# Attention, then experts: the order of GpSimd's instructions, token numbers inside the sorted rows, two heads per block for the last queries, and fp16 scalars in the bias layer

## The chip, the cores and the metric

The kernel runs on one core of a Trainium2 chip. The engines of the core work side by side, each through its own queue of instructions: TensorE (PE, matmuls; PEld its weight loads), VectorE (DVE), ScalarE (ACT), GpSimd (POOL) and SyncE (SP). In this kernel POOL and SP also issue the DMA transfers. The metric is the time of one execution on the device in microseconds; lower is better.

## What is computed

Eight batches of eight heads with 576 tokens and 64 values per head go through softmax attention with an additive bias; the bias comes from a small two-layer network on the logarithm of the distance of two tokens. The result of each token, a row of 512 values, then goes through one of eight experts, which its domain id names.

```python
rel = pos[:, None] - pos[None, :]
x = (log1p(abs(rel)) / log1p(maximum(pos[:, None], 1)))[..., None]
bias = maximum(x @ w1 + b1, 0) @ w2            # hidden width 32, one value per head
scores = q @ k.T / sqrt(64) + bias             # per batch and head, 576 x 576
attn = softmax(scores) @ v
x = attn.transpose(0, 2, 1, 3).reshape(4608, 512)
for e in range(8):                             # domain_id: 4608 numbers 0..7
    m = domain_id == e
    out[m] = maximum(x[m] @ w1[e], 0) @ w2[e]  # 512 -> 1024 -> 512
```

## The kernel before, in words

**Setup** (`_setup_constants`, L67 to L108) builds a table L of logarithms of distances (128 partitions: 32 hidden units for each of four query positions), a `slope` column for each group of four queries and the negated bias `nb`. **The bias phase** (`_phase_bias`) runs over nine blocks of 64 queries. For each, VectorE makes 16 tiles `hr` (L126: a window of L times a column of `slope`, then the maximum with `nb`), TensorE multiplies each by W2BIG into `eb` (L136; L141 for the last 64 keys, twice, once for each half of the partitions), and ScalarE moves `eb` out as exp(bias), or as the plain bias for some parts (L150, L153, L156).

**Routing** (`_phase_route`) gives each token a slot: expert e owns slots 640e to 640e + 639, in five chunks of 128, and a loop for an overflow beyond that is not entered with these data. VectorE counts in a chain of small operations that begins with the matmul `app` (L207) and ends with `posi` (L276), the slot of each token. Forty indirect DMAs on GpSimd (L287) then scatter the token numbers into `fire_perm`, an array in HBM, and SyncE loads that back as `sidx` (L292).

**Attention** (`_Attention.run`) takes 21 units for each batch: TensorE computes the scores of 128 keys by 512 queries for two heads (or some other 1024-wide piece), ScalarE takes the exp (L412), VectorE multiplies it by exp(bias) (L417), and TensorE multiplies with v (`av`) into `pu`. `norm` divides by the sum. Five indirect DMAs on GpSimd (L477) put the batch's rows, in fp16, into their slots in `fire_x`. q, k and v of batch b + 2 are ordered from HBM at unit 1 of batch b, also through GpSimd; a DMA from an fp32 array into an fp16 tile converts. p = 4 in `av` and `norm` are the last 64 queries.

**The experts** (`_phase_moe`): one DMA on SyncE fetches the 640 rows of an expert (`xg`, L578), TensorE transposes them (L559), then the first layer (`hps`, L601), Relu on ScalarE (L605) and the second layer (`ops`, L566). VectorE copies `ops` to `res` (L569, four buffers) and GpSimd scatters `res` to the output (L570) by `sidx`. Weights of experts 0 to 2 are loaded during attention, those of experts 3 to 6 by eight DMAs in a row at the start of the experts, those of expert 7 after expert 0.

The order of instructions on PE, DVE and ACT is that of the program. On POOL and SP the scheduler chooses it.

Of the kernel before, what the change touches and what calls it, by code (L numbers as in the profile page):

```python
# [9 lines left out]
F32 = mybir.dt.float32  # L10
# [6 lines left out]
P = 128  # L17
S = 576
# [12 lines left out]
PAD = 1 << 20  # L31

# [23 lines left out]
def _no_order(tc, key, inst):  # L56

    ins = inst.ins if hasattr(inst, "ins") else inst
    tc.declare_no_dep(ins, group=key, reason="rows of one permutation")
    tc.add_to_no_dep_group(key, ins)  # L60


def _setup_constants(tc, G, w1, b1, w2):
# [12 lines left out]
    nc.sync.dma_start(out=w1col, in_=bass.AP(tensor=w1.tensor, offset=0, ap=[[0, 4], [1, 32], [1, 1]]))  # L76
    G.nb1 = cst.tile([P, 1], F32, tag="nb1", name="nb1")
    nc.sync.dma_start(out=G.nb1, in_=bass.AP(tensor=b1.tensor, offset=0, ap=[[0, 4], [1, 32], [1, 1]]))
    nc.vector.tensor_scalar(out=G.nb1, in0=G.nb1, scalar1=-1.0, scalar2=None, op0=AO.mult)
# [9 lines left out]
    si = cst.tile([P, NGR], I32, tag="si", name="si")  # L89
    li = G.tmp.tile([P, W4 + W1], I32, tag="li", name="li")  # L90
    for g in range(4):
        pg = slice(32 * g, 32 * g + 32)

        nc.gpsimd.iota(si[pg, 0:128], base=4 * g, channel_multiplier=0, pattern=[[1, 4], [16, 32]])
        nc.gpsimd.iota(si[pg, 128:144], base=512 + g, channel_multiplier=0, pattern=[[4, 16]])
        nc.gpsimd.iota(li[pg, 0:W4], base=-(C4 + 4 * g), channel_multiplier=0, pattern=[[1, W4]])
        nc.gpsimd.iota(li[pg, W4:], base=-(C1 + 512 + g), channel_multiplier=0, pattern=[[1, W1]])
    G.slope = cst.tile([P, NGR], F32, tag="slope", name="slope")
    nc.vector.tensor_copy(out=G.slope, in_=si)
    nc.vector.tensor_scalar(out=G.slope, in0=G.slope, scalar1=1.0, scalar2=None, op0=AO.max)  # L100
    nc.scalar.activation(out=G.slope, in_=G.slope, func=AF.Ln, bias=1.0, scale=1.0)
    nc.vector.reciprocal(out=G.slope, in_=G.slope)
    nc.vector.tensor_scalar(out=G.slope, in0=G.slope, scalar1=w1col[:], scalar2=None, op0=AO.mult)
    lf = G.tmp.tile([P, W4 + W1], F32, tag="lf", name="lf")
    nc.vector.tensor_copy(out=lf, in_=li)
    nc.vector.scalar_tensor_tensor(out=lf, in0=lf, scalar=-1.0, in1=lf, op0=AO.mult, op1=AO.max)
    G.L4 = cst.tile([P, W4 + W1], F16, tag="L4", name="L4")
    nc.scalar.activation(out=G.L4, in_=lf, func=AF.Ln, bias=1.0, scale=1.0)  # L108


def _phase_bias(tc, G):
# [3 lines left out]
    with tc.tile_pool(name="fsb", bufs=1, side="right") as fsb, \  # L115
         tc.tile_pool(name="fps", bufs=1, space=bass.MemoryType.PSUM) as fps:
        for ib in range(9):
            hrl = []
            for k16 in range(16):
# [3 lines left out]
                else:  # L123
                    m, c0 = 128 + k16, W4 + C1 - 4 * k16
                hr = fsb.tile([P, S], F16, tag="hr", name="hr", bufs=36)
                nc.vector.tensor_scalar(out=hr, in0=G.L4[:, c0: c0 + S],  # L126
                                        scalar1=G.slope[:, m: m + 1], scalar2=G.nb1[:],
                                        op0=AO.mult, op1=AO.max)
                hrl.append(hr)
            for jcs in ((0, 1), (2, 3), (4,)):  # L130
                eb = fps.tile([P, 2, 512], F32, tag="eb", name="eb", bufs=3)
                for k16 in range(16):
                    for lj, jc in enumerate(jcs):
                        hr = hrl[k16]
                        if jc < 4:
                            nc.tensor.matmul(out=eb[:, lj, 32 * k16: 32 * k16 + 32],  # L136
                                             lhsT=rap(hr, jc, [[4, 128]]),
                                             rhs=G.W2BIG[:, 0:32], start=True, stop=True)
                        else:
                            for h2 in range(2):  # L140
                                nc.tensor.matmul(  # L141
                                    out=eb[64 * h2: 64 * h2 + 64, lj, 32 * k16: 32 * k16 + 32],
                                    lhsT=hr[:, 512:576], rhs=G.W2BIG[:, 0:32], start=True, stop=True)
                ebv = eb.rearrange("p l (i h) -> p l h i", h=8)
                i0 = 64 * ib
                if jcs[0] == 4:
                    for h2 in range(2):
                        o = G.biasR[64 * h2: 64 * h2 + 64, :, i0: i0 + 64] if ib < 8 else \
                            G.biasRL[64 * h2: 64 * h2 + 64]
                        nc.scalar.activation(out=o, in_=ebv[64 * h2: 64 * h2 + 64, 0, h2::2, :],  # L150
# [16 lines left out]
def _phase_route(tc, G, moe_domain_id):  # L167
# [8 lines left out]
    G.perm_dram = nc.dram_tensor("fire_perm", (NSLOT, 1), I32, kind="Internal").ap()  # L176
# [563 lines left out]
```

## Time and profile before

| | |
|---|---|
| median of 3 runs | 527.84 us (526.59 to 532.48) |
| the profiled execution | 523.68 us, its span 522.0 us |
| busy in the span | PE 373.6 us (72%), DVE 260.3 (50%), ACT 231.1 (44%), POOL 202.0 (39%) |
| mean granted clock of TensorE | 0.896 of full speed |
| stages | setup to 16 us, bias to 70, routing to 88, attention to 321, experts to 514, end 522 |

The profile was taken in one execution, and its times are counted from the start of its span. Busy shares are means over stages that have different limits, so the table alone does not say what a change in one stage is worth.

### The profile page before, as it was taken

The numbers are of one execution on the slowest core, as the hardware profiler recorded it, in microseconds if no ns is written. First come the engines' busy times: TensorE is split into PE (matmuls) and PEld (weight loads), VectorE is DVE, ScalarE is ACT, GpSimd is POOL, SyncE is SP. The second block draws the span as 40 slices with busy tenths as digits, with TensorE's granted clock in tenths as the row PEclk, the third lists the DMA queues.
The fourth block names the chain that finished last, engine by engine and source line by source line (L and its number), as shares of the span: only waits on it lengthen the run. The fifth ranks groups of instructions, "written<-read, shape, count | busy, mean of one in ns | idle before, by whom it ended". The sixth has DMA issues, their size and how long they took to land. (4 is left out here: it accounts for less than half of the span.)

```text
span 522.0 us, 10886 instructions
## 1 busy us (share of the span) xinstructions
PE 373.6 (72%) x4578; PEld 235.3 (45%) x4578; DVE 260.3 (50%) x572; ACT 231.1 (44%) x290; POOL 202.0 (39%) x238
## 2 busy tenths in 40 slices
PE   0578844311298988889898977079639999999992
PEld 0366733100055555465555544055425566566550
DVE  5899985100369695777768674013022422422411
ACT  1444521000388987889697875021402143143140
POOL 9740445777606546543403042603013303313312
PEclk9999999555599999999897989579959999999997
DMA  0999987000992999979401010899998313102211
GB/s 3 155 233 366 319 123 131 2 0 0 99 155 53 161 203 149 151 124 114 77 3 46 4 46 21 160 241 241 215 246 206 112 50 123 69 22 88 81 39 73
DMA packets 79034, 61.39 MB, mean 118 GB/s; under 512 B 23558, under 2 KB 71430, under 8 KB 78984
## 3 DMA queue, kind: packets, MB, share of 16 engines
q0 software_dynamic: 56576, 45.12, 49.7%
q1 hardware_dynamic: 22408, 15.57, 10.8%
q8 instruction: 36, 0.59, 0.4%
q14 instruction: 14, 0.11, 0.1%
HBM read 67.17 MB, written 25.49 MB: 177 GB/s over the span
## 5 line engine op out<-in xcount | busy, mean ns | idle before, releaser
L412 ACT ACTIVATE e<-sc 128x1024 f16<-128x1024 f32 x168 | 156.7, 998 | 93.5 <-remote 67.2
L605 ACT ACTIVATE hT<-hps 128x640 f16<-128x640 f32 x64 | 45.1, 704 | 137.8 <-PE hps L601 136.2
L570 POOL DMA_INDIRECT out_dram<-res,sidx x40 | 39.5, 988 | 132.6 <-DVE res L569 131.9
L566 PE MATMUL ops<-w2e,hT 128*128 128x512 f16 x320 | 71.5, 383 | 0.0
L601 PE MATMUL hps<-xT,w1e 128*128 128x320 f16 x512 | 71.2, 300 | 0.0
L385 PE MATMUL sc<-qkT 64*128 64x512 f16 x256 | 54.3, 407 | 22.7 <-ACT e L412 16.7
L477 POOL DMA_INDIRECT fire_x<-xt,posi x32 | 34.4, 1076 | 81.2 <-DVE xt L459 71.0
L569 DVE COPY res<-ops 128x512 f32<-128x512 f32 x40 | 27.7, 691 | 76.2 <-PE ops L566 51.0
L417 DVE TENSOR_TENSOR e<-e,biasM 128x1024 f16<-128x1024 f16 x96 | 63.4, 685 | 3.3 <-ACT e L412 3.0
L601 PEld LDWEIGHTS <-w1e 128*128 128x128 f16 x512 | 50.3, 98 | 20.7
L136 PE MATMUL eb<-W2BIG,hr 128*128 128x32 f16 x576 | 36.0, 196 | 25.8 <-DVE hr L126 18.8
L433 PE MATMUL pu<-vext,e 128*128 128x65 f16 x1024 | 53.0, 199 | 0.0
L126 DVE TENSOR_SCALAR hr<-L,slope,nb 128x576 f16<-128x576 f16 x144 | 51.6, 435 | 1.7 <-ACT L L108 1.7
L561 DVE COPY xT<-pxt 128x512 f16<-128x512 f16 x40 | 15.8, 421 | 65.8 <-PE pxt L559 64.1
L566 PEld LDWEIGHTS <-hT 128*128 128x128 f16 x320 | 31.3, 99 | 36.8 <-issue 1.4
L287 POOL DMA_INDIRECT fire_perm<-nidx,posi x40 | 38.7, 969 | 21.0 <-issue 21.0
L433 PEld LDWEIGHTS <-e 128*128 128x128 f16 x1024 | 46.2, 102 | 0.0
L367 DVE COPY qkT<-pt 128x1024 f16<-128x1024 f16 x32 | 21.8, 683 | 47.7 <-remote 43.5
L136 PEld LDWEIGHTS <-hr 128*128 128x128 f16 x576 | 26.5, 117 | 34.7 <-DVE hr L126 17.6
L429 PE MATMUL pu<-vrag,e 128*128 128x130 f16 x128 | 29.9, 234 | 13.1 <-DVE xl L470 7.9
L559 PE MATMUL pxt<-idn,xg 128*128 128x128 f16 x160 | 15.1, 235 | 33.6 <-DMA xg<-fire_x 18.1
L345 PE MATMUL pt<-idn,qn 128*64 128x128 f16 x256 | 15.3, 249 | 27.1 <-DVE qkT L367 14.3
(123 smaller groups left out, 407.6 us busy)
## 6 DMA issues: line engine op xcount, KB each, us to landing
fire_x<-zero SPq DMA_DIRECT2D x1, 9984.0 KB, 37.0
w1e<-in_moe_w_dram POOLq DMA_DIRECT2D x8, 1024.0 KB
w2e<-in_moe_w_dram POOLq DMA_DIRECT2D x8, 1024.0 KB
xg<-fire_x SPq DMA_DIRECT2D x8, 640.0 KB, 8.6
qn<-in_q_dram POOLq DMA_DIRECT2D x8, 512.0 KB
kn<-in_k_dram POOLq DMA_DIRECT2D x8, 512.0 KB
vst<-in_v_dram POOLq DMA_DIRECT2D x8, 512.0 KB
fire_perm<-nidx,posi POOLq DMA_INDIRECT x40
```

What stands on the lines that cost most here:

```text
L126: nc.vector.tensor_scalar(out=hr, in0=G.L4[:, c0: c0 + S], scalar1=G.slope[:, m: m + 1], scalar2=G.nb1[:], op0=AO.mult, op1=AO.max)
L136: nc.tensor.matmul(out=eb[:, lj, 32 * k16: 32 * k16 + 32], lhsT=rap(hr, jc, [[4, 128]]), rhs=G.W2BIG[:, 0:32], start=True, stop=True)
L287: _no_order(tc, "slots", nc.gpsimd.indirect_dma_start(out=G.perm_dram[:, :], out_offset=bass.IndirectOffsetOnAxis(ap=G.posi[0:n, c:c + 1], ...
L385: mm(out=sc[:, h2, :], lhsT=self.qkT[b, p][hs[h2], 1, 128 * c: 128 * c + 128], rhs=self.qkT[b, p][hs[h2], 0, :], start=not raw, stop=True)
L412: nc.scalar.activation(out=ef[:, 0:n], in_=sf[:, 0:n], func=AF.Exp, bias=0.0, scale=0.125)
L417: self.nc.vector.tensor_tensor(out=job[0], in0=job[0], in1=job[1], op=AO.mult)
L433: mm(out=self.pu[:, c // 2, o + 65 * h2: o + 65 * h2 + 65], lhsT=self.e[b, ("m", p, j)][:, h2, 128 * c: 128 * c + 128], rhs=vx[:, 2 * p + ...
L477: _no_order(self.tc, "x_rows", self.nc.gpsimd.indirect_dma_start(out=self.x_dram[:, :], out_offset=bass.IndirectOffsetOnAxis(ap=self.G.pos ...
L566: nc.tensor.matmul(out=ops_, lhsT=hT[:, fc, t0: t0 + 128], rhs=w2e[:, fc, :], start=(fc == 0), stop=(fc == 7))
L570: _no_order(tc, "out_rows", nc.gpsimd.indirect_dma_start(out=out[:], out_offset=bass.IndirectOffsetOnAxis(ap=idx, axis=0), in_=res[:], in_ ...
L601: nc.tensor.matmul(out=hps[:, hf, 0:HC], lhsT=w1e[:, dc, 128 * fc: 128 * fc + 128], rhs=xT[:, dc, HC * hf: HC * hf + HC], start=(dc == 0), ...
L605: nc.scalar.activation(out=hT[:, fc, :].rearrange("p (a b) -> p a b", a=2), in_=hps[:, :, 0:HC], func=AF.Relu, bias=0.0, scale=1.0)
```

## The change

On **GpSimd**, a helper `_Issue` fixes the order of loads, token iotas, weights and scatters to that of the program; scatters that follow each other stay free among themselves. The **forty L287 scatters** go, and with them `fire_perm` and `sidx`: rows of `fire_x` are now 514 wide, and the last four bytes hold the token number, which a small iota on GpSimd writes into `xt` and `xl` (`new_rows`). Slots that no token fills get PAD with the zero fill. The out scatter takes its row numbers from `xg` itself.

`xg` is fetched as **five DMAs of 128 rows** per expert, two experts ahead. **Weights** of expert e + 3 are loaded behind the first out scatter of expert e; `res` has six buffers. The program orders the weights of experts 0, 1 and 2 at unit 13 of batches 1, 2 and 3, as before; GpSimd now keeps to that place.

For the **last 64 queries**, one matmul takes two heads of the queries as its 128 rows and two heads of v: 20 in place of 36 per batch; `norm` divides 128 x 512 in one operation. In the **bias phase**, 27 of the 144 `hr` tiles move to ScalarE (Relu with scale and bias), the other 117 take their two pointer scalars as fp16 copies, and the last 64 keys need one matmul per tile, not two. **Setup** uses fewer, wider iotas, takes the absolute value on ScalarE, and does the table in two parts.

```diff
+class _Issue:
+    def __call__(self, inst):
+        ins = _ins(inst)
+        for before in self.free or ([self.fixed] if self.fixed is not None else []):
+            self._behind(ins, before)
+        self.fixed, self.free = ins, []
+        return inst
+    def scatter(self, inst):
+        ins = _ins(inst)
+        if self.fixed is not None:
+            self._behind(ins, self.fixed)
+        self.free.append(ins)
+        return inst
...
+    G.slope16 = cst.tile([P, NGR], F16, tag="slope16", name="slope16")
+    nc.vector.tensor_copy(out=G.slope16, in_=G.slope)
...
+    nc.scalar.activation(out=lf[:, W4:], in_=li[:, W4:], func=AF.Abs, bias=gs[:, 2:3], scale=1.0)
+    nc.scalar.activation(out=G.L4[:, W4:], in_=lf[:, W4:], func=AF.Ln, bias=1.0, scale=1.0)
...
-                nc.vector.tensor_scalar(out=hr, in0=G.L4[:, c0: c0 + S],
-                                        scalar1=G.slope[:, m: m + 1], scalar2=G.nb1[:],
-                                        op0=AO.mult, op1=AO.max)
+                if k16 in (3, 8, 13):
+                    nc.scalar.activation(out=hr, in_=G.L4[:, c0: c0 + S], func=AF.Relu,
+                                         bias=G.pb1[:], scale=G.slope[:, m: m + 1])
+                else:
+                    nc.vector.tensor_scalar(out=hr, in0=G.L4[:, c0: c0 + S],
+                                            scalar1=G.slope16[:, m: m + 1], scalar2=G.nb16[:],
+                                            op0=AO.mult, op1=AO.max)
...
-    for bb in range(B):
-        for t in range(NT):
-            n = 128 if t < 4 else 64
-            c = NT * bb + t
-            _no_order(tc, "slots", nc.gpsimd.indirect_dma_start(
-                out=G.perm_dram[:, :],
-                out_offset=bass.IndirectOffsetOnAxis(ap=G.posi[0:n, c:c + 1], axis=0),
-                in_=nidx[0:n, bb, t:t + 1], in_offset=None))
...
+            out = self.pu[:, h2, o: o + 130].rearrange("p (q d) -> p q d", q=2)
+            mm(out=out, lhsT=ex[:, 0, 64 * q: 64 * q + 128],
+               rhs=vr[:, q: q + 2, 65 * h2: 65 * h2 + 65], start=True, stop=False, skip_group_check=True)
+            for j in range(4):
+                l0 = 256 * (j % 2) + 64 * q
+                mm(out=out, lhsT=self.e[b, ("l", j // 2)][:, h2, l0: l0 + 128],
+                   rhs=vx[:, 2 * q + h2: 2 * q + h2 + 3: 2, j, :], start=False, stop=(j == 3),
+                   skip_group_check=True)
...
+    def new_rows(self, tag, n, c, base, step):
+
+        t = self.G.asb.tile([n, c, XW], F16, tag=tag, name=tag, bufs=2)
+        self.G.issue(self.nc.gpsimd.iota(t[:, :, DM:].bitcast(I32), base=base, channel_multiplier=step,
+                                         pattern=[[1, c], [0, 1]]))
+        return t
...
-        xg = msb.tile([P, NCH, DM], F16, tag="xg", name="xg", bufs=3)
-        nc.sync.dma_start(out=xg, in_=x_dram[e * CAP: e * CAP + CAP, :]
-                          .rearrange("(k p) d -> p k d", p=128))
...
+            xg = msb.tile([P, XW], F16, tag="xg", name="xg", bufs=4 * NCH)
+            r0 = e * CAP + 128 * kk
+            nc.sync.dma_start(out=xg, in_=x_dram[r0: r0 + 128, :])
...
-        if e == 0:
-            for e2 in range(G.NW, min(E, G.NW + G.NW2)):
-                G.wts[e2] = _load_expert(nc, G.wsb2, moe_w1, moe_w2, e2, G.NW2)
...
-            second(hT, 128 * kk, w2e, G.sidx[:, e * NCH + kk, :])
-        if e + G.NW + G.NW2 < E:
-            G.wts[e + G.NW + G.NW2] = _load_expert(nc, G.wsb, moe_w1, moe_w2, e + G.NW + G.NW2, G.NW)
+            second(hT, 128 * kk, w2e, xgs[e][kk][:, DM:])
+            if kk == 0 and e + G.NW < E:
+                e2 = e + G.NW
+                pool, n = (G.wsb2, G.NW2) if e < G.NW2 else (G.wsb, G.NW)
+                G.wts[e2] = _load_expert(nc, pool, moe_w1, moe_w2, e2, n, G.issue)
```

On GpSimd, after routing, this stands before (qn, ql, kn, kl and vst are q, k and v of a batch and their last 64 tokens, vrag the last tokens of v; the first qn is that of batch 2):

```order
L287 DMA fire_perm<-nidx,posi 9984x1 x40
L323 DMA qn<-in_q_dram 128x8x256
L323 DMA kn<-in_k_dram 128x8x256
L331 DMA vst<-in_v_dram 128x8x256
L323 DMA qn<-in_q_dram 128x8x256
```

And this now, on the same engine in the same place:

```order
L301 MEMSET pb 128x672
L359 DMA qn<-in_q_dram 128x8x256
L362 DMA ql<-in_q_dram 64x8x64
L359 DMA kn<-in_k_dram 128x8x256
L362 DMA kl<-in_k_dram 64x8x64
L369 DMA vst<-in_v_dram 128x8x256
L376 DMA vrag_134<-in_v_dram 64x4x64 x2
L520 IOTA xt 128x4
L359 DMA qn<-in_q_dram 128x8x256
```

The loads of batch 2, and those of batch 3 that begin in the last row, follow the memory fills of routing; nothing that takes `posi` stands ahead of them.

On GpSimd, at the start of the experts, the last rows of weights and the out scatters stand so before (w1e and w2e are the two layers of an expert):

```order
L543 DMA w2e<-in_moe_w_dram 128x8x512
L570 DMA out_dram<-res,sidx 4608x512 x4
L541 DMA w1e<-in_moe_w_dram 128x4x1024
L570 DMA out_dram<-res,sidx 4608x512
L543 DMA w2e<-in_moe_w_dram 128x8x512
L570 DMA out_dram<-res,sidx 4608x512 x35
```

And so now, from the last sorted rows on:

```order
L526 DMA fire_x<-xl,posi 9984x514
L617 DMA out_dram<-res,xg 4608x512
L592 DMA w1e<-in_moe_w_dram 128x4x1024
L594 DMA w2e<-in_moe_w_dram 128x8x512
L617 DMA out_dram<-res,xg 4608x512 x5
L592 DMA w1e<-in_moe_w_dram 128x4x1024
L594 DMA w2e<-in_moe_w_dram 128x8x512
L617 DMA out_dram<-res,xg 4608x512 x5
```

The weights come in pairs, with five out scatters between two pairs; before, the eight loads stood ahead of the first out scatter.

## Rows read from the trace of the kernel before

**Rows 1.** Windows: us, busy (instructions) PE, PEld, DVE, ACT, POOL; PEclk, DMA share, GB/s

```profile
0.00:16.00 16.00, 0.00 (x0) 0.00 (x0) 8.35 (x11) 3.25 (x4) 14.72 (x39) 1.00 0.15 11
16.00:70.00 54.00, 44.23 (x866) 34.97 (x866) 52.96 (x149) 25.32 (x54) 21.58 (x25) 1.00 1.15 258
91.00:139.00 48.00, 7.52 (x60) 3.86 (x57) 3.00 (x5) 2.08 (x3) 35.20 (x37) 0.50 0.12 12
139.00:321.00 182.00, 158.40 (x2511) 96.28 (x2511) 134.87 (x278) 152.65 (x164) 68.45 (x73) 0.95 0.67 96
179.00:202.00 23.00, 21.01 (x360) 13.10 (x359) 17.76 (x38) 19.90 (x22) 9.43 (x10) 1.00 1.18 189
321.00:345.00 24.00, 4.60 (x77) 4.03 (x74) 4.18 (x11) 0.00 (x0) 11.40 (x13) 0.59 0.76 157
345.00:514.00 169.00, 151.47 (x974) 90.80 (x972) 41.63 (x76) 45.07 (x64) 41.28 (x42) 0.96 0.51 130
```

**Rows 2.** Timeline of ScalarE, 86 to 160 us: start, busy, operation, [idle before <-releaser]

```profile
88.59 1.02 ACT L412 ACTIVATE e<-sc 128x1024 f16<-128x1024 f32 x1 [17.84 <-remote]
...
116.20 1.02 ACT L412 ACTIVATE e<-sc 128x1024 f16<-128x1024 f32 x1 [20.87 <-remote]
139.42 4.87 ACT L412 ACTIVATE e<-sc 128x1024 f16<-128x1024 f32 x5 [22.19 <-remote]
...
156.94 3.77 ACT L412 ACTIVATE e<-sc 128x1024 f16<-128x1024 f32 x4 [0.65 <-PE sc L391]
```

**Rows 3.** Timeline of GpSimd, 80 to 140 us

```profile
82.87 1.05 POOL L287 DMA_INDIRECT fire_perm<-nidx,posi  x1 [9.15 <-issue]
...
133.50 0.97 POOL L323 DMA_DIRECT2D qn<-in_q_dram  x1
```

**Rows 4.** Groups by line and shape: count, busy us, mean ns, idle before

```profile
L126 DVE TENSOR_SCALAR hr<-L,slope,nb 128x576 f16<-128x576 f16 x144 | 51.6, 435 | 1.7 <-ACT L L108 1.7
...
L153 ACT ACTIVATE biasM<-eb 128x768 f16<-128x768 f32 x16 | 13.0, 811 | 25.9 <-PE eb L136 25.9
...
L156 ACT ACTIVATE biasM<-eb 128x256 f16<-128x256 f32 x16 | 6.1, 379 | 0.0
L150 ACT ACTIVATE biasR<-eb 64x256 f16<-64x256 f32 x16 | 6.0, 378 | 0.1
L342 DVE COPY vext<-vst 128x2048 f16<-128x2048 f16 x8 | 5.5, 686 | 0.0
```

**Rows 5.** Timeline of TensorE, 68 to 72 us

```profile
69.87 0.21 PE L207 MATMUL app<-rowtot,ut 128*128 128x8 f16 x2
```

**Rows 6.** Timeline of VectorE, 68 to 83 us

```profile
81.81 0.18 DVE L276 CAST posi<-posf 128x40 int32<-128x40 f32 x1
```

**Rows 7.** Timeline of ScalarE, end of attention

```profile
317.70 3.29 ACT L412 ACTIVATE e<-sc 128x1024 f16<-128x1024 f32 x4 [0.15 <-PE sc L385]
```

**Rows 8.** Timeline of ScalarE, 250 to 262 us

```profile
256.75 2.86 ACT L412 ACTIVATE e<-sc 128x1024 f16<-128x1024 f32 x3 [2.63 <-remote]
```

**Rows 9.** Timeline of GpSimd, 320 to 340 us

```profile
327.72 0.90 POOL L477 DMA_INDIRECT fire_x<-xl,posi  x1 [0.30 <-issue]
328.61 0.83 POOL L541 DMA_DIRECT2D w1e<-in_moe_w_dram  x1
```

**Rows 10.** Timeline of TensorE, 340 to 360 us

```profile
342.36 2.81 PE L559 MATMUL pxt<-idn,xg 128*128 128x128 f16 x20 [18.14 <-DMA xg<-fire_x]
344.96 9.21 PE L601 MATMUL hps<-xT,w1e 128*128 128x320 f16 x64
```

**Rows 11.** Timeline of VectorE, 380 to 400 us

```profile
385.21 0.69 DVE L569 COPY res<-ops 128x512 f32<-128x512 f32 x1 [21.39 <-DMA out_dram<-res,sidx]
```

**Rows 12.** Timeline of TensorE, 430 to 480 us

```profile
436.22 8.86 PE L601 MATMUL hps<-xT,w1e 128*128 128x320 f16 x64
...
455.57 8.86 PE L601 MATMUL hps<-xT,w1e 128*128 128x320 f16 x64
```

**Rows 13.** Timeline of GpSimd, end of the experts

```profile
512.76 0.98 POOL L570 DMA_INDIRECT out_dram<-res,sidx  x1 [0.74 <-DVEq L622]
```

More of the change, by code (lines that the diff above doesn't have):

```diff
@@ L31 @@
 PAD = 1 << 20
+XW = DM + 2
 NT = 5
@@ L56, in _no_order, with _ins, __init__, _behind @@
 def _no_order(tc, key, inst):
-    ins = inst.ins if hasattr(inst, "ins") else inst
+    ins = _ins(inst)
     tc.declare_no_dep(ins, group=key, reason="rows of one permutation")
     tc.add_to_no_dep_group(key, ins)
+def _ins(inst):
+    return inst.ins if hasattr(inst, "ins") else inst
+class _Issue:
+    def __init__(self, tc):
+        self.tc, self.fixed, self.free = tc, None, []
+    def _behind(self, ins, before):
+        self.tc.add_manual_dep(ins, before.name, mybir.DependencyInfo(
+            mybir.DependencyClass.NoSync, mybir.DependencyReason.DATA), reason="issue order")
+    def __call__(self, inst):
[5 more added lines that the diff above has]
+    def scatter(self, inst):
+        ins = _ins(inst)
+        if self.fixed is not None:
+            self._behind(ins, self.fixed)
+        self.free.append(ins)
+        return inst
 def _setup_constants(tc, G, w1, b1, w2):
@@ new lines, in _setup_constants @@
+    nc.gpsimd.iota(si[:, 128:144], base=512, channel_multiplier=0, pattern=[[4, 16]])
+    pf = cst.tile([P, 2], F32, tag="pf", name="pf")
+    nc.vector.tensor_copy(out=pf[:, 0:1], in_=pi)
+    g1 = cst.tile([P, 1], F32, tag="g1", name="g1")
+    nc.vector.tensor_scalar(out=g1, in0=pf[:, 0:1], scalar1=32.0, scalar2=None, op0=AO.is_ge)
+    for lim in (64.0, 96.0):
+        nc.vector.tensor_scalar(out=pf[:, 1:2], in0=pf[:, 0:1], scalar1=lim, scalar2=None, op0=AO.is_ge)
+        nc.vector.tensor_tensor(out=g1, in0=g1, in1=pf[:, 1:2], op=AO.add)
@@ new lines, in _setup_constants @@
+    gs = cst.tile([P, 3], F32, tag="gs", name="gs")
+    nc.vector.tensor_scalar(out=gs[:, 0:1], in0=g1, scalar1=4.0, scalar2=None, op0=AO.mult)
+    nc.vector.tensor_scalar(out=gs[:, 1:2], in0=g1, scalar1=-4.0, scalar2=None, op0=AO.mult)
+    nc.vector.tensor_scalar(out=gs[:, 2:3], in0=g1, scalar1=-1.0, scalar2=None, op0=AO.mult)
+    lf = G.tmp.tile([P, W4 + W1], F32, tag="lf", name="lf")
+    G.L4 = cst.tile([P, W4 + W1], F16, tag="L4", name="L4")
+    nc.scalar.activation(out=lf[:, 0:W4], in_=li[:, 0:W4], func=AF.Abs, bias=gs[:, 1:2], scale=1.0)
@@ new lines, in _setup_constants @@
+    nc.scalar.activation(out=G.L4[:, 0:W4], in_=lf[:, 0:W4], func=AF.Ln, bias=1.0, scale=1.0)
+    G.slope = cst.tile([P, NGR], F32, tag="slope", name="slope")
+    nc.vector.tensor_scalar(out=G.slope[:, 0:128], in0=si[:, 0:128], scalar1=gs[:, 0:1], scalar2=1.0,
+                            op0=AO.add, op1=AO.max)
+    nc.vector.tensor_scalar(out=G.slope[:, 128:], in0=si[:, 128:], scalar1=g1[:], scalar2=1.0,
+                            op0=AO.add, op1=AO.max)
+    nc.scalar.activation(out=G.slope, in_=G.slope, func=AF.Ln, bias=1.0, scale=1.0)
@@ L80, in _setup_constants @@
+    nc.vector.reciprocal(out=G.slope, in_=G.slope)
+    nc.vector.tensor_scalar(out=G.slope, in0=G.slope, scalar1=w1col[:], scalar2=None, op0=AO.mult)
+    G.slope16 = cst.tile([P, NGR], F16, tag="slope16", name="slope16")
+    nc.vector.tensor_copy(out=G.slope16, in_=G.slope)
+    G.nb16 = cst.tile([P, 1], F16, tag="nb16", name="nb16")
+    nc.vector.tensor_copy(out=G.nb16, in_=G.nb1)
     w2sb = cst.tile([HID, 8], F32, tag="w2sb", name="w2sb")
@@ L139, in _phase_bias @@
                         else:
[L140 to L143, printed above, removed]
+                            nc.tensor.matmul(out=eb[0:64, lj, 32 * k16: 32 * k16 + 32],
+                                             lhsT=hr[:, 512:576],
+                                             rhs=G.W2BIG[:, 0:32], start=True, stop=True)
                 ebv = eb.rearrange("p l (i h) -> p l h i", h=8)
```

174 lines of the change are left out of this document (76 added, 98 removed).

## The prediction

> **What bounds the kernel now.** I read the windows first, cut where the stages change [rows 1]. In 16–70 us, the bias phase, VectorE is busy for 52.96 of 54 us: it makes the hr tiles and sets the pace, ScalarE works for only 25.32. In 91–139 us nothing is near its limit: TensorE 7.52 us, VectorE 3.00, ScalarE 2.08, the DMA engines at 0.12, and only GpSimd is busy, 35.20 of 48 us. That is the largest hole of the profile. From 139 to 321 us, attention runs with ScalarE at 152.65 and TensorE at 158.40 of 182 us: a dense stage with two engines near the limit. 321–345 us is the passage to the experts (TensorE 4.60 of 24 us). The experts take 345–514 us with TensorE busy for 151.47 of 169, so some 17 us are missing there as well.
>
> The timelines name the holes. On ScalarE the first exp stands at 88.59 us; then come single ones, and waits of 20.87 and 22.19 us before those at 116.20 and 139.42 us, both put down to "remote", a signal of another engine that the profile can't name [rows 2]. On GpSimd the forty fire_perm scatters run from 82.87 us, and the first load of q for batch 2 stands right behind them at 133.50 us, so a scatter takes (133.50 − 82.87)/40 = 1.27 us [rows 3]. The hole has two covers: signals arrive late while GpSimd issues scatters back to back, and the data of batch 2 isn't ordered until they are over. The change takes away both, so their shares needn't be told apart for the sum.
>
> **The change, part by part.** The sum is made against the profiled execution, 523.68 us (a span of 522.0 and 1.7 around it); the median of the three runs, 527.84, is 4.2 us above it, and I carry these 4.2 along.
>
> *Setup and bias.* A tile of hr on VectorE costs 51.6/144 = 0.358 us [rows 4], 16 of them 5.73 us for one 64-query block; 13 cost 4.65 us. ScalarE evacuates a block in 2 × 0.811 + 2 × 0.379 + 2 × 0.378 = 3.14 us [rows 4]. It gets three hr tiles; no row shows one, but 576 elements lie between the 256 of 0.379 us and the 768 of 0.811 us, on the line between them 0.65 us, at the bounds 0.38 and 0.81. So ScalarE needs 3.14 + 3 × 0.65 = 5.09 us for a block (4.3 to 5.6) and becomes the engine that paces it, where VectorE did with 5.73: 9 × 0.64 = 5.8 us less. TensorE's 16 matmuls fewer in each block lie under that. The setup's iotas shrink (GpSimd is busy for 14.72 of the first 16 us [rows 1]), but Abs and Ln on ScalarE now stand in a row, with a third table load, and the four W2BIG operations stand ahead of hr. I take +1 to −2 us, 0 as the middle. The first block's hr tiles on ScalarE and bubbles between blocks cost about 1 us, and the last block's evacuations don't hold up TensorE, which gives some 2 us back; both are guesses inside the bounds. So app comes at 69.87 − 7 = 63 us [rows 5], from 60 (bounds above, setup gain) to 68.
>
> The fp16 pointer scalars: hr moves 576/0.358 = 1,610 elements per us, the copy vext, also 16-bit in SBUF, 2,048/0.686 = 2,985 [rows 4]. If the scalars were what keeps hr at half that pace, a tile would fall to about 0.2 us and 13 to 2.6. But ScalarE, at 5.09, sets the block's pace either way: this edit is worth nothing after the first block, and 13 × 0.16 = 2.1 us ahead of the first evacuation at the most. I take 0. The Trainium skill, "DVE: scalar operands, raw-bit mode, write accounting and state across instructions", section "Scalar operands", says that a [P,1] scalar is converted to fp32 on load and that a bf16 scale costs the same as an fp32 one; by that hr stays at 0.358 us, and the sum below is 449; with hr at 0.2 it would be 447. The Trainium skill, "VectorE: DVE Perf Modes", section "The perf-mode tier table", lets a 16-bit tensor-scalar operation in SBUF run at the copy's pace; the hr row, at half of it, doesn't bear that out for fp32 scalars, and no run of the kernel before has fp16 ones.
>
> *Route.* The VectorE chain from app to posi is unchanged: 69.87 to 81.99, 12.1 us [rows 5, 6]. From posi to the first exp it is 6.6 us, part of it under the scatters [rows 2, 6]; without them I take 5 (4 to 6.6). The first exp: 63 + 12.1 + 5 = 80, **8.6 us earlier**.
>
> *The forty scatters and the order on GpSimd.* With them go 50.6 us of GpSimd, and the loads of batch 2 and batch 3 are issued ahead of all that waits for posi, as the order shows. Batch 0 runs now from 88.59 to 156.94, 68.4 us; its last 17 units took 17.52 us, 1.03 each [rows 2], so 21 of them take 21.6. **−46.7 us.** Batches 1 to 7 took 320.99 − 156.94 = 164.05 us, 23.4 each [rows 2, 7]. I leave that. The delay that follows the five fire_x scatters of each batch (2.63 us at 256.75 [rows 8]) stays, since these scatters stay. The token iotas, two small ones per batch, stand on GpSimd behind the loads, where they wait for nothing that is late; cost 0, at most as long as a scatter each, 2.5 us per batch, if GpSimd were full, and it is busy for 68.45 of 182 us [rows 1].
>
> *Last queries and norm.* 16 matmuls fewer per batch; at the stage's mean of 158.40/2511 = 63 ns that is 1.0 us per batch, 8 in all, if TensorE paces, and 0 if ScalarE does. ScalarE's units stand back to back in the timeline [rows 2], so I take **−1**. The wider norm operations leave VectorE, at 134.87 of 182 us, as free as it was.
>
> *Weights and DMA.* By their shapes in fp16, q, k and v of a batch are 1.8 MB, the weights of an expert 2.1 MB and a batch's sorted rows 0.6 MB. In batches 1, 2 and 3 the change asks for all three, 4.5 MB in 23.4 us. In 179–202 us of before the queues moved 189 GB/s × 23 us = 4.35 MB, while ScalarE and TensorE worked at the stage's usual rate (19.90 and 21.01 of 23 us) [rows 1]. The queues have done this already, so I take 0; the loads also have a whole batch of lead.
>
> *To the experts.* The last fire_x scatter is issued at 327.72; behind it eight loads of weights, from 328.61 on, take the queues, and the first transposes wait for xg until 342.36, hps until 344.96 [rows 9, 10]. Now xg has the queues to itself and comes in five pieces: 0.66 MB at 189 GB/s is 3.5 us, and a start of about 1.5, so 5 in place of 13.7. **−8.7**, bounds 0 (as long as before) and −10. The 1,028-byte rows in place of 1,024 are a little longer; I take 0.
>
> *Experts.* From hps at 344.96 to the end of the last scatter at 513.74 it takes 168.8 us [rows 10, 13]. The steady pitch is 455.57 − 436.22 = 19.35 [rows 12], and 8 of these are 154.8. What is missing is mostly one wait: at 385.21 res waits 21.39 us for an out scatter [rows 11] that is behind the eight loads on the queues. With two loads per expert, issued behind its first out scatter, and six res buffers instead of four, it goes: **−14.0**. Forty xg DMAs on SyncE's queue in place of eight lie under TensorE's 19.35 us; uncovered, they would cost only their landing, some 5 us per expert.
>
> Sum: −8.6 − 46.7 − 1 − 8.7 − 14.0 = −79.0; 523.68 − 79.0 = 444.7 profiled, and with the 4.2 **449 us**. Its own range is 438 to 458, from the bounds above.
>
> **The rivals.**
> *A, the queues fall behind (457–475 us).* The weights of three experts all move into batches 1 to 3; before, a part came ahead of the scatters, when the DMA share was 1.15 in 16–70 us. In 179–202 us that share was 1.18 [rows 1], so there was nothing left over. If q and k of batches 3 to 5 come 3 to 8 us late, 9 to 24 us are added. For it: that share. Against: ScalarE kept its pace in just this stretch, and the fixed order puts the loads ahead of scatters.
>
> *B, the late signals stay (about 495 us).* The "remote" waits might not come from the scatters; then the hole of 46.7 us stays: 449 + 46.7. Against: it begins and ends with the forty, the DMA share is 0.12 and all other engines are idle [rows 1 to 3]. That is also the case that the change doesn't do what it says.
>
> *C, slower than before (over 533 us).* In a fixed order an early instruction that waits holds up all behind it. If each batch's load stood behind a scatter that waits for VectorE, the 1.8 MB would be exposed: 9.4 us at 189 GB/s, 56 us for batches 2 to 7; the 2.1 MB of eight experts cost 11.1 us each, 89 in all. Together 145 us. It decides from 79 us on, over half of all this exposed; at the full price it gives 594. Against: in the order the loads stand a batch and more ahead of their use, and what they wait for, TensorE's transposes of two batches earlier, is over by then.
>
> *D, more than the sum (432–438).* TensorE paces attention more than I take it (up to −7 more), hr at double pace and a shorter setup (−4), fewer late signals after fire_x (up to 2 us per batch).
>
> **How the numbers follow.** Forecast 0.62; A 0.14; B 0.04; C 0.03; D 0.14; further down 0.03. The range of 432 to 470 takes in the forecast's own, D, and most of A, about 0.86 by these numbers and less for what I have not thought of. Within 1% (5.3 us, about what a measurement of this kernel can tell from no change): 0.02; slower 0.03; faster 0.95.
>
> **What would show it.** In the profile after: no hole between the first exp (about 80 us) and batch 1; seven batches of 23.4 us; last exp near 265; hps within 15 us of it; hps pitches of 19.35 with no wait of res for an out scatter. hr on VectorE at 0.358 us or at 0.2 tells what the scalars do, and ScalarE's idle time in the bias phase whether it paces it. I am wrong if q or k landings end waits in batches 3 to 5 (A), or if long "remote" waits remain without the forty (B).

## The result and the profile after

The changed kernel takes 464.23 us (median of 4 runs, 463.16 to 465.77) against 527.22 before: a ratio of 0.880 (95% interval 0.872 to 0.887). The time lies in the range that was given, 432 to 470, and 15 us above the forecast of 449. The profiled execution has a span of 464.2 us, so nearly the whole difference lies inside the profile. (The median is not above the profiled run, 465.77, this time; the 4.2 us carried along for that weren't there.)

The windows of the changed kernel, cut at its own stages (columns as in [rows 1]):

```profile
14.00:68.00 54.00, 35.23 (x720) 30.85 (x721) 42.05 (x120) 46.77 (x82) 6.04 (x13) 1.00 1.24 192
68.00:102.00 34.00, 4.69 (x76) 4.15 (x77) 14.71 (x46) 0.00 (x0) 0.17 (x1) 1.00 0.47 75
102.00:286.00 184.00, 159.62 (x2500) 96.06 (x2500) 142.06 (x271) 155.38 (x168) 78.36 (x98) 0.99 0.77 116
302.00:455.00 153.00, 149.66 (x967) 89.92 (x966) 40.53 (x74) 45.04 (x64) 47.04 (x49) 0.99 0.68 153
```

Attention is one dense stage of 184 us now and the experts have TensorE busy for 149.66 of 153 us; the holes of 91–139 and of expert 1 [rows 1, 11] are gone. But a new one stands ahead of attention: from 68 to 102 us ScalarE does nothing. Its timeline, from the last hr tiles to the last exp:

```profile
62.37 2.39 ACT L178 ACTIVATE hr<-L,pb,slope 128x576 f16<-128x576 f16 x3
...
102.99 2.85 ACT L451 ACTIVATE e<-sc 128x1024 f16<-128x1024 f32 x3 [35.02 <-PE sc L430]
...
124.21 6.60 ACT L451 ACTIVATE e<-sc 128x1024 f16<-128x1024 f32 x7 [0.59 <-PE sc L430]
...
281.91 3.29 ACT L451 ACTIVATE e<-sc 128x1024 f16<-128x1024 f32 x4 [0.15 <-PE sc L424]
```

Batch 0 takes 124.21 − 102.99 = 21.2 us (68.4 before [rows 2]) and batches 1 to 7 take 161.0. Only the start is late: the first exp stands at 103 us, not at 80. VectorE's timeline, then SyncE's, say why:

```profile
84.99 0.18 DVE L240 CAST domf<-dom 128x40 f32<-128x40 int32 x1 [26.34 <-DMA dom<-in_moe_domain_id_dram]
...
98.47 0.18 DVE L329 CAST posi<-posf 128x40 int32<-128x40 f32 x1
```

```profile
21.64 0.64 SPq L743 DMA_DIRECT2D fire_x<-zero  x1
22.34 52.24 SPq L236 DMA_DIRECT2D dom<-in_moe_domain_id_dram  x1
```

Routing begins with the domain ids, and VectorE waits 26.34 us for them. Their second load is queued on SyncE behind the zero fill of fire_x; the queue stands on it for 52 us. In the kernel before it stood in the same place, but for 31.70 us, and VectorE took the ids with no wait as soon as its hr tiles were done (the fill, issued at 27.35, had landed 37.0 us later, at 64.4):

```profile
28.04 31.70 SPq L183 DMA_DIRECT2D dom<-in_moe_domain_id_dram  x1
```

```profile
67.57 0.17 DVE L187 CAST domf<-dom 128x40 f32<-128x40 int32 x1
```

What changed is the pace of the fill. Four views of the DMA queues follow, each of a window in which next to nothing but the fill ran: before (45 to 60 us), after (45 to 75), and two of the experiments below (45 to 55 with rows of 1,088 bytes, 40 to 50 with pieces of 6,168 bytes).

```profile
DMA packets 5576, 5.75 MB, mean 383 GB/s; under 512 B 0, under 2 KB 5573, under 8 KB 5573
```

```profile
DMA packets 5297, 5.51 MB, mean 184 GB/s; under 512 B 0, under 2 KB 5292, under 8 KB 5292
```

```profile
DMA packets 3154, 3.47 MB, mean 347 GB/s; under 512 B 0, under 2 KB 3151, under 8 KB 3151
```

```profile
DMA packets 652, 4.03 MB, mean 403 GB/s; under 512 B 0, under 2 KB 0, under 8 KB 650
```

With rows of 1,028 bytes in place of 1,024 the same fill runs at half the rate. The rest of the run is close to the forecast; TensorE's timeline at the experts and VectorE's idle time ahead of res (the first line of what it waited for):

```profile
297.50 2.19 PE L606 MATMUL pxt<-idn,xg 128*128 128x128 f16 x16 [9.32 <-DMA xg<-fire_x]
...
300.52 10.92 PE L648 MATMUL hps<-xT,w1e 128*128 128x320 f16 x64
...
321.93 8.86 PE L648 MATMUL hps<-xT,w1e 128*128 128x320 f16 x64
...
341.27 3.97 PE L648 MATMUL hps<-xT,w1e 128*128 128x320 f16 x28
```

```profile
  PE ops L613: 52.0, 40
```

The pitch is 341.27 − 321.93 = 19.34 us, as in [rows 12], and res waits for TensorE alone, all forty times.

### The profile page after: what moved, and what is told of

The parts are those of the page before. It is cut to its first block, busy times and chain, and to the rows that moved or that the text cites. A ratio compares the mean times of both kernels' runs of the same rounds, so it can differ in the third digit from the quotient of the medians.

```text
span 464.2 us, 10320 instructions
## 1 busy us (share of the span) xinstructions
PE 355.1 (76%) x4306; PEld 224.9 (48%) x4306; DVE 247.9 (53%) x538; ACT 254.5 (55%) x321; POOL 151.1 (33%) x201
## 5 line engine op out<-in xcount | busy, mean ns | idle before, releaser
L617 POOL DMA_INDIRECT out_dram<-res,xg x40 | 40.0, 999 | 115.0 <-DVE res L616 108.1
L648 PE MATMUL hps<-xT,w1e 128*128 128x320 f16 x512 | 72.9, 304 | 0.0
L424 PE MATMUL sc<-qkT 64*128 64x512 f16 x256 | 50.6, 390 | 8.5 <-ACT e L451 8.5
L191 PE MATMUL eb<-W2BIG,hr 128*128 128x32 f16 x576 | 26.9, 194 | 31.6 <-ACT hr L178 15.5
L473 PE MATMUL pu<-vext,e 128*128 128x65 f16 x1024 | 50.7, 194 | 0.0
L473 PEld LDWEIGHTS <-e 128*128 128x128 f16 x1024 | 43.9, 98 | 0.1
L181 DVE TENSOR_SCALAR hr<-L,slope,nb 128x576 f16<-128x576 f16 x117 | 41.7, 435 | 2.6 <-PE eb L195 2.5
L191 PEld LDWEIGHTS <-hr 128*128 128x128 f16 x576 | 22.3, 116 | 35.6 <-ACT hr L178 18.0
L359 POOL DMA_DIRECT2D qn<-in_q_dram x8 | 7.4, 923 | 90.3 <-PE pt L384 90.3
L424 PEld LDWEIGHTS <-qkT 64*128 64x128 f16 x256 | 13.8, 93 | 31.5 <-issue 24.8
L469 PEld LDWEIGHTS <-e 128*128 128x128 f16 x128 | 12.4, 97 | 31.1 <-issue 18.6
```

The source lines that it names most:

```text
L181: nc.vector.tensor_scalar(out=hr, in0=G.L4[:, c0: c0 + S], scalar1=G.slope16[:, m: m + 1], scalar2=G.nb16[:], op0=AO.mult, op1=AO.max)
L191: nc.tensor.matmul(out=eb[:, lj, 32 * k16: 32 * k16 + 32], lhsT=rap(hr, jc, [[4, 128]]), rhs=G.W2BIG[:, 0:32], start=True, stop=True)
L424: mm(out=sc[:, h2, :], lhsT=self.qkT[b, p][hs[h2], 1, 128 * c: 128 * c + 128], rhs=self.qkT[b, p][hs[h2], 0, :], start=not raw, stop=True)
L469: mm(out=self.pu[:, c // 2, o: o + 130], lhsT=er[:, p % 2, 128 * c: 128 * c + 128], rhs=vr[:, p, :], start=True, stop=False, skip_group_ch ...
L473: mm(out=self.pu[:, c // 2, o + 65 * h2: o + 65 * h2 + 65], lhsT=self.e[b, ("m", p, j)][:, h2, 128 * c: 128 * c + 128], rhs=vx[:, 2 * p + ...
L617: inst = nc.gpsimd.indirect_dma_start(out=out[:], out_offset=bass.IndirectOffsetOnAxis(ap=idx.bitcast(I32), axis=0), in_=res[:], in_offset ...
```

## Experiments

Each time is of one run unless a number of runs stands with it; the changed kernel's is 464.2. Experiments 1 to 4, 5 to 8 and 9 to 11 share a chip each, and the changed kernel itself ran on another occasion. What chips can do to a time shows in two kernels that hardly differ: 1 took 446.28 us on the first chip, 7 took 446.14 on the second. The third differs more: the kernel before took 524.7 and 520.2 us on the first two and 498.1 on the third.

**1. Domain ids ahead of the fill** (`dom_first`).

```diff
+            _load_domains(tc, G, moe_domain_id)     # the memset and both loads of dom2, moved up from routing
             at = _Attention(tc, G, q, k, v, x_dram)
             at.start()
```

> Both loads of the domain ids are issued ahead of the zero fill, nothing else changes. Theory F (the route chain starts late because its input stands behind the slow fill on SyncE's queue): rowtot is ready when the bias phase ends, app follows the last matmul of the bias phase (67 us in place of 86.6), the first exp stands at 84 us (103 before), and the run takes 445 us (443 to 449). Rival R (the fill holds up more than this one load: q, k and v of the first batches, or the sorted rows that wait for it): the first exp moves by less than 10 us and the run takes over 454.

446.28 us (4 runs, 446.09 to 446.95; ratio to before 0.850, 0.847 to 0.852). TensorE's and ScalarE's timelines:

```profile
66.95 0.21 PE L266 MATMUL app<-rowtot,ut 128*128 128x8 f16 x2
```

```profile
83.25 2.86 ACT L457 ACTIVATE e<-sc 128x1024 f16<-128x1024 f32 x3 [15.42 <-PE sc L436]
```

App stands at 66.95 (86.56 in the changed kernel) and the first exp at 83.25: theory F. The place of one 4 KB load on a queue cost 18 us.

**2. Rows of 1,088 bytes, the load still behind the fill** (`rows1088`).

```diff
+XD = 544                                            # fire_x, xt, xl and zero are 544 wide; 514 are fetched
-            zero = G.cst.tile([P, 1, XW], F16, tag="zero", name="zero")
+            zero = G.cst.tile([P, 1, XD], F16, tag="zero", name="zero")
```

> Rows of fire_x are 1088 bytes long (a multiple of 64) in place of 1028; the domain load stays behind the fill on SyncE's queue. Theory A (a row length that leaves rows unaligned makes the writes slow): alone on the queues the fill moves over 350 GB/s again (180 in the changed kernel), the domain ids land near 62 us, hidden behind the bias phase, and the run takes 446 us. Rival L (any piece over 1024 bytes is slow): the fill stays near 180 GB/s, the first exp at 103 us or later, the run at 464 to 469.

444.61 us; the fill ran at 347 GB/s, where the 1,028-byte fill of experiment 1, on the same chip, ran at 179 (45 to 75 us). VectorE took the ids ahead of the end of the bias phase:

```profile
61.92 0.18 DVE L242 CAST domf<-dom 128x40 f32<-128x40 int32 x1 [3.47 <-DMA dom<-in_moe_domain_id_dram]
```

Theory A: it is not the size over 1,024 bytes. Rows of 1,028 bytes begin at any multiple of 4, rows of 1,088 at multiples of 64; whether the start of a row or its length decides, these runs don't tell apart.

**3. The same rows in pieces of six** (`long_fill`).

```diff
+                nc.sync.dma_start(
+                    out=x_dram.rearrange("(p c k) d -> p c (k d)", p=P, k=6),
+                    in_=zero.rearrange("p o k d -> p o (k d)").to_broadcast([P, NSLOT // P // 6, 6 * XW]))
```

> The fill writes the same 1028-byte rows, six at a time, in contiguous pieces of 6168 bytes; the domain load stays behind it. Theory A (the cost is at the unaligned ends of each piece): a sixth of the ends, so the fill is over by 60 us, app is at 67 us and the run takes 446 us. Rival W (the cost comes per byte or per row of this fill, however it is cut): the run stays at 464 and the first exp at 103 us.

448.78 us, the fill at 403 GB/s, and VectorE took the ids at 60.4 us with no wait: theory A again, the cost goes with the number of pieces and not with the bytes or rows. The Trainium skill, "DMA: Bandwidth & Descriptors", section "How a descriptor splits into AXI transactions", lets a piece that doesn't begin on a boundary of 256 bytes cost further beats, since its first transaction starts at the boundary below. It says so of reads, and these rows are written. The direction agrees; the size doesn't: one transaction more on four or five is an estimate of some 25%, the runs show a factor of 2, and rows of 1,088 bytes, most of which don't begin on such a boundary either, a tenth.

**4. Twelve scatters in the middle of batch 0** (`flood12`).

```diff
+            if (b, ui) == (0, 2):
+                self.flood(12)      # 12 indirect scatters of 4-byte rows to an array that nothing reads
```

> The changed kernel with 12 more indirect scatters of 4-byte rows, into an array that nothing reads, behind the loads of batch 2 and ahead of those of batch 3 on GpSimd. Theory S (signals between the engines come late while GpSimd issues scatters back to back): for 12 x 1.27 = 15 us, the exps of batch 0 come singly with waits put down to remote, and the run is 12 to 15 us longer, 477 to 480. Rival O (the hole of the kernel before was the late order of batch 2's loads): these loads are out already, those of batch 3 have 20 us of lead left; batch 0 takes its 21 us and the run stays within 3 us of 464.

480.51 us. Batch 0 takes 138.62 − 105.14 = 33.5 us in place of 21.2, 12.3 more for 15.2 us of scatters (and the first exp of this run stood 2.2 us later):

```profile
105.14 2.86 ACT L451 ACTIVATE e<-sc 128x1024 f16<-128x1024 f32 x3 [37.08 <-PE sc L430]
...
112.23 2.85 ACT L451 ACTIVATE e<-sc 128x1024 f16<-128x1024 f32 x3 [1.73 <-PE sc L424]
...
123.15 1.02 ACT L451 ACTIVATE e<-sc 128x1024 f16<-128x1024 f32 x1 [6.21 <-remote]
126.10 1.94 ACT L451 ACTIVATE e<-sc 128x1024 f16<-128x1024 f32 x2 [1.93 <-PE sc L424]
...
138.62 7.44 ACT L451 ACTIVATE e<-sc 128x1024 f16<-128x1024 f32 x8 [0.59 <-PE sc L430]
```

Theory S has it, and rival O has fallen: the data were there, so scatters alone make such a hole, 12.3/15.2 = 0.81 of their time here and 46.7/50.6 = 0.92 before. How they hold the other engines up is not shown: the profile puts the long waits down to "remote" or names nothing, and that signals come late is a reading of this. Ordinary loads don't do it: in the changed kernel GpSimd issues twelve of them from 101.8 to 114.2 us while ScalarE's units stand back to back.

**5. Eight loads of weights at once** (`at_once`).

```diff
+        if e == 0:
+            for e2 in range(G.NW, G.NW + G.NW2):
+                G.wts[e2] = _load_expert(nc, G.wsb2, moe_w1, moe_w2, e2, G.NW2, G.issue)
-            if kk == 0 and e + G.NW < E:
...
```

> The changed kernel with the weights of experts 3 to 6 loaded by eight transfers in a row at the start of the experts, as before; five xg pieces per expert and six res buffers stay. Theory Q (the eight loads fill the queues, and xg and the out scatters wait behind them): from the last exp to the first hps 22 to 24 us in place of 15.3, res waits for an out scatter at expert 1 for about 9 us of TensorE's time, and the run takes 478 to 485. Rival B (four res buffers and the one-piece xg made the waits): both stay as in the changed kernel and the run takes 464 to 467.

482.6 us. From the end of the last exp (289.1) to hps at 311.51 it is 22.4 us, 15.3 in the changed kernel, and one pitch is 357.26 − 332.24 = 25.0 us. Together 12.8 of the 17 us by which the span is longer; the rest is a first exp that came 3.6 us later in this run and small things. TensorE's timeline and the waits of res:

```profile
332.24 8.86 PE L651 MATMUL hps<-xT,w1e 128*128 128x320 f16 x64
...
357.26 8.86 PE L651 MATMUL hps<-xT,w1e 128*128 128x320 f16 x64
```

```profile
  DMA out_dram<-res,xg: 6.1, 1
```

Theory Q, and rival B has fallen. At expert 1 the wait is back but is 6.1 us long, not 9; before, it was 21.39 [rows 11], for which TensorE stood idle for 12.33. That the six buffers take up the rest is argued, not shown.

**6. The last queries as before** (`dom_p4_old`, on top of 1).

```diff
-            h2, q = c // 2, 2 * (c % 2)
...
+                    mm(out=self.pu[0:64, c // 2, o + 65 * h2: o + 65 * h2 + 65],
+                       lhsT=self.e[b, ("l", j // 2)][:, h2, l0: l0 + 64],
+                       rhs=vx[:, 2 * c + h2, j, :], start=False, stop=(h2 == 1 and j == 3),
+                       skip_group_check=True)
```

> Domain ids ahead of the fill, and the last 64 queries as before, with 36 matmuls per batch in place of 20. Theory P (TensorE paces part of a batch, and the two-head blocks gave the 0.4 us per batch by which the changed kernel's batches are shorter): a batch takes 23.4 us in place of 23.0 and the run 448 to 450. Rival E (ScalarE alone paces, the two-head blocks are hidden): a batch stays at 23.0 and the run at 445 to 447.

443.65 us, and 446.14 for the next kernel on the same chip, which differs in the blocks (and in the scalars, which do nothing). From first to last exp it takes 178.9 us with 36 matmuls and 181.4 with 20: theory P has fallen. But these totals mix granted clocks: batches 1 to 3 took 71.5 us at 0.95 here and 68.8 at 1.00 there, batch 7 took 19.8 at 1.00 and 22.8 at 0.93. Where both had 1.00, in batches 4 to 6, the windows of `dom_p4_old` and then of `dom_fp32` are:

```profile
177.10:243.50 66.40, 60.13 (x1024) 37.27 (x1023) 52.52 (x100) 58.53 (x64) 31.58 (x30) 1.00 0.57 87
```

```profile
175.40:244.00 68.60, 60.25 (x974) 36.89 (x975) 54.43 (x106) 58.26 (x63) 24.08 (x30) 1.00 0.60 92
```

So in these three batches the two-head blocks cost 2.2 us, 0.7 per batch, rather than hide; it is one run each. The groups, in the same order:

```profile
L475 PE MATMUL pu<-vrag,e 128*128 128x130 f16 x128 | 29.3, 229 | 9.2 <-DVE xl L514 4.5 <-DVE xt L503 3.5 <-DVE rz L513 1.1
...
L514 DVE TENSOR_TENSOR xl<-pu,rz 64x512 f16<-64x512 f32 x8 | 5.5, 683 | 0.6
```

```profile
L475 PE MATMUL pu<-vrag,e 128*128 128x130 f16 x128 | 29.2, 228 | 9.3 <-DVE xl L518 7.3 <-DVE xt L503 1.8
...
L518 DVE TENSOR_TENSOR xl<-pu,rz 64x256 f16<-64x256 f32 x16 | 6.7, 421 | 0.9
```

The block saves matmuls, but its norm is two multiplications of 421 ns and two reciprocals of 178 where there were 683 and 196: 0.32 us more per batch, half of the 0.7, while the next matmuls wait for the only pu buffer. That this is the cause is argued from the waits for xl and its reciprocal (7.3 against 4.5 and 1.1), not shown.

**7. fp32 pointer scalars** (`dom_fp32`, on top of 1).

```diff
-                                            scalar1=G.slope16[:, m: m + 1], scalar2=G.nb16[:],
+                                            scalar1=G.slope[:, m: m + 1], scalar2=G.nb1[:],
```

> Domain ids ahead of the fill, and the pointer scalars of hr in fp32 as before. Theory N (the scalar's type does nothing): hr on VectorE stays at 0.357 us a tile and the run at 445 to 447. Rival H (fp16 scalars are faster): a tile takes longer with fp32 ones, over 0.37 us, the bias phase grows by some us where VectorE ends it, and the run takes 448 or more.

446.14 us. The groups of hr in the changed kernel (fp16 scalars), then in this one:

```profile
L181 DVE TENSOR_SCALAR hr<-L,slope,nb 128x576 f16<-128x576 f16 x117 | 41.7, 435 | 2.6 <-PE eb L195 2.5
L178 ACT ACTIVATE hr<-L,pb,slope 128x576 f16<-128x576 f16 x27 | 21.5, 858 | 0.2
```

```profile
L181 DVE TENSOR_SCALAR hr<-L,slope,nb 128x576 f16<-128x576 f16 x117 | 41.6, 434 | 3.5 <-PE eb L195 3.5
```

41.7 and 41.6 us for 117 tiles: theory N. The Trainium skill, "DVE: scalar operands, raw-bit mode, write accounting and state across instructions", section "Scalar operands", has a scale in bf16 cost the same as one in fp32. With fp16 in place of bf16 the two runs agree.

**8. Two hr tiles on ScalarE in place of three** (`dom_two_act`, on top of 1).

```diff
-                if k16 in (3, 8, 13):
+                if k16 in (5, 11):
```

> Domain ids ahead of the fill, and two hr tiles of each block on ScalarE (numbers 5 and 11) in place of three. Theory T (ScalarE paces the bias phase at 5.64 us a block, of which 2.39 are its three hr tiles): a block takes 5.0 to 5.2 us, app stands at 63 us in place of 67, and the run takes 442. Rival U (the waits of TensorE for hr tiles of ScalarE set the block, wherever they stand): a block stays at 5.6 us and the run at 445 to 447.

461.5 us, 15 longer than `dom_first` and than 7, which ran on the same chip, though the bias phase did what was expected: app at 62 us, a block every 5.00 us. Rival U has fallen, and so has the forecast. The timelines of VectorE and of GpSimd:

```profile
14.58 43.27 DVE L181 TENSOR_SCALAR hr<-L,slope,nb 128x576 f16<-128x576 f16 x126
```

```profile
19.49 39.14 POOL L382 DMA_DIRECT2D vrag<-in_v_dram  x2 [1.93 <-DMA vst<-in_v_dram]
58.67 0.53 POOL L748 MEMSET zero<- 128x512 f16 x1
...
131.39 1.04 POOL L532 DMA_INDIRECT fire_x<-xt,posi  x1 [17.24 <-DMA fire_x<-zero]
```

Two issues that take 1.3 us otherwise took 39.14, until VectorE's 126 tiles, made with no pause, were over. The fill began at 59 us in place of 21, ran beside the loads of batches 2 and 3, and held up the first sorted rows. The kernel before has a smaller case: VectorE makes its 144 tiles without a pause, from 16.00 to 67.6 us, and one issue stood to 68.1 where others of its kind take 0.8:

```profile
59.18 8.95 POOL L541 DMA_DIRECT2D w1e<-in_moe_w_dram  x1 [27.80 <-PE eb L141]
```

**9. The same, with the fill ordered first** (`two_act_early`).

```diff
+            zero = G.cst.tile([P, 1, XW], F16, tag="zero", name="zero")   # and the constants of routing
...
             at = _Attention(tc, G, q, k, v, x_dram)
             at.start()
```

> As the kernel with two hr tiles on ScalarE, but GpSimd fills the zero tile and the constants of routing ahead of its loads, so that the zero fill is ordered near 7 us. Theory G (in that kernel one GpSimd issue stood for 38.5 us while VectorE made hr without a pause, so the fill began at 59 us in place of 21 and held up the loads of batches 2 and 3 and the sorted rows): the fill is over by 70 us whatever GpSimd does later, there is no hole in batches 0 and 1, and the run takes 440 to 443. Rival V (the order of hr tiles on ScalarE disturbs attention in another way): holes of 10 us stay in batches 0 and 1 and the run takes over 455.

437.44 us, a little under theory G; no hole in batches 0 and 1. (Batches 1 to 7 took 156.0 us at a granted clock of 1.00; those of 7, on another chip, took 160.2 and had 0.93 in the last.) In this run no issue of GpSimd stood, so that the late fill did the harm is shown, but not that this kernel stands up to a late issue.

**10 and 11. Routing out of the way** (`spread1088`; `best` adds 8 and 9).

```diff
-            _phase_route(tc, G, moe_domain_id)
+            route = _phase_route(tc, G, moe_domain_id)   # now yields after each operation behind app
+            next(route)
             at.head()
...
                 def late(b, ui):
+                    for _ in range(2):
+                        next(route, None)
```

> Domain ids first, rows of 1088 bytes, routing spread over batch 0 as above; hr tiles and the fill's place on GpSimd as in the changed kernel. Theory: app at 67 us, the first exp at 71 to 72, the run 434 to 437. Rival as above: batch 0 takes 27 us or more and the run 441 or more.

> The kernel of the run before in this list, with rows of 1088 bytes and with routing taken out of the way: VectorE makes the prefix sums of the domain ids ahead of app, then the copies for the first scores, and the rest of routing a few operations per unit of batch 0. Theory: app at 62 us, the first exp near 67 in place of 83, some 2 us given back in batch 0 where VectorE has 6 us more to do; the run takes 429 to 433. Rival (VectorE is full in batch 0, and posi comes late for the first sorted rows): batch 0 takes 27 us or more and the run 436 or more.

434.12 us, and for `best` 431.29 (4 runs, 430.87 to 431.54). ScalarE's timeline of `best`, and the group of one load on GpSimd from 8 to 70 us:

```profile
68.38 2.85 ACT L487 ACTIVATE e<-sc 128x1024 f16<-128x1024 f32 x3 [5.40 <-PE sc L466]
...
85.33 1.02 ACT L487 ACTIVATE e<-sc 128x1024 f16<-128x1024 f32 x1 [3.80 <-PE sc L460]
...
95.65 7.44 ACT L487 ACTIVATE e<-sc 128x1024 f16<-128x1024 f32 x8 [0.58 <-PE sc L466]
```

```profile
L398 POOL DMA_DIRECT2D kl<-in_k_dram x2 | 28.2, 14117 | 5.7 <-DMA kn<-in_k_dram 5.7
```

The first exp came 14.9 us earlier than in 1, and 11.8 earlier than in 9, on the same chip (80.21). Batch 0 took 27.3 us (26.8 in `spread1088`), so 6 came back, as the rival had it; the other 5.7 are what `best` has over 9. The run is still as short as the theory had it, because batches 1 to 7 took 156.1 us, as in 9, where those of 1 took 163.4 with a granted clock that fell to 0.95 in batches 1 to 3 and to 0.93 in batch 7. So the theory's time came out, but its 2 us for batch 0 did not. An issue stood again, for 27.5 us, and did no harm, since nothing urgent was behind it. `best` is faster than both kernels; its ratio to before is 0.865 (0.862 to 0.868) in its own job, where the kernel before took only 498.06.

**12. The kernel before once more** (`before_again`), since it took 498 to 527 us in these jobs.

> The kernel before, unchanged, to see how far its hole varies: its median was 498 to 527 us in the jobs of this study, on different chips, where the changed kernel and its variants kept within 3 us of what was expected. Theory S (late signals under the forty scatters): where the run is shorter, the first exps after the routing stand closer together, and the length from the first exp to batch 1 (68.4 us in the first profile) takes up the whole difference. Rival: the difference lies in all stages alike.

526.04 us, and 159.08 − 90.08 = 69.0 us from the first exp to batch 1 (68.4 in the first profile). The run was as long as in the first profile, so nothing is told apart; why the kernel before took 498 in one job stays open.

## Why the prediction came out as it did

The sum was 79 us off the time before, and 58 were found in the profile. Against its own steps:

- **The forty scatters**: −46.7 forecast; batch 0 went from 68.4 to 21.2 us, −47.2. Right in size, and `flood12` shows which of the two covers it was: the scatters themselves, not the late order of the loads.
- **To the experts**: −8.7 forecast; 285.2 to 300.5 is 15.3 us, 24.0 before: −8.7.
- **Experts**: −14.0 forecast; 300.52 to 457.5 is 157.0, 168.8 before: −11.8. The first expert took 21.4 us in place of 19.35: its first layer ran for 10.92 us in place of 8.86, at a granted clock of 0.81 (300.5 to 311.5 us), behind a passage (286 to 302) with 0.66 in which TensorE was busy for 5.34 of 16 us.
- **Batches 1 to 7**: unchanged in the sum; they took 161.0 in place of 164.05. The one microsecond that stood for the last queries is not where it came from, by experiment 6. Before, the granted clock was 0.93, 0.87 and 0.93 in 248 to 272, 272 to 298 and 298 to 321 us; after, it was 1.00 in every batch from the second of these seven on. That the 3 us come from there is likely, not tested.
- **Bias**: app was to come at 63; the phase ended at 67.2. An hr tile took 0.80 us on ScalarE (21.5/27), the upper bound, not 0.65, and ScalarE waited 0.47 us in each block for eb, so a block took 5.64 us, not 5.09. Mis-sized by 4 us, and covered here by the wait for the ids.
- **The fp16 scalars**: 0 forecast and 0 measured, in experiment 7. The comparison that left the question open, 1,610 elements of hr per us against 2,985 of a copy, leaves out what an operation costs at any length: in the changed kernel a copy of 8 elements (`ovn`) takes 0.17 us, and hr's tiles are 576 elements long, the copy's 2,048.
- **The step that failed**: "The 1,028-byte rows in place of 1,024 are a little longer; I take 0." It was applied to the fetch of xg alone. The zero fill has the same rows, ten megabytes of them, and SyncE's queue held an input of the route chain behind it; the sum had no term for it, and the chain from app to posi was costed without asking when its first input comes. Instead the fill ran at 184 GB/s in place of 383, the first exp came at 103 us in place of 80, and the run was 18 us longer than it need have been, by experiment 1; experiments 2 and 3 show that the rows of the fill do it. With the load moved the run is 446, beside the 449 forecast, of which 4.2 were an offset that didn't appear: the 4 us of the bias phase stand against these, so part of that agreement is luck.

Rival A had queues that fall behind, in batches 3 to 5; no wait for q or k stands there. The queues were full, but in the bias phase, and it was a load of 4 KB that was late. That 464 lies in the range is therefore luck: the upper end was there for A, and another hole filled it. B and C did not happen.

## What to carry to other kernels

A change of a row's length is a change to every transfer of such rows; cost the largest first, then look at what is queued behind it. Ask of each stage when its first input lands, also where it has always been early: the fill ahead of the ids had landed at 64.4 us, and they were wanted at 67.57. And where one engine is made to run with no pause, order what others wait for ahead of it: in three of these kernels an issue of GpSimd stood until VectorE's unbroken run was over.

## What the runs showed of the hardware that was not expected

- A fill of 1,028-byte rows runs at 184 GB/s (179 in experiment 1), of 1,024 at 383, of 1,088 at 347, and of 6,168-byte pieces of the same 1,028-byte rows at 403.
- In two of the three kernels where VectorE made 126 hr tiles with no pause, one DMA issue of GpSimd stood for 38.5 and 27.5 us, to VectorE's end (58.6 against 57.9 us, and 58.9 against 58.5); in the kernel before, one stood for 8.95. The Trainium skill, "SBUF — State Buffer", section "SBUF: two separate sides", has a lock that VectorE in some of its fast modes holds and without which GpSimd can't write the descriptors of a DMA. That these issues end with VectorE's tiles agrees with it. But GpSimd got through other issues during the same run of tiles, and in the third kernel through all of them; what decides it these runs don't show.
- Back-to-back indirect scatters on GpSimd cost the other engines 0.8 to 0.9 of their time in batch 0 (12.3 of 15.2 us, 46.7 of 50.6); twelve direct loads from 101.8 to 114.2 us cost nothing that shows.
